# Output gates in 96 packets, constants made by GpSimd, the first weight fold in eight pieces, two PSUM accumulator tiles, and new ranks

## The chip, the cores and the metric

The kernel runs on one core of one Trainium2 chip. The metric is the device time of one execution in microseconds (us); the median of three runs is what a change is measured by. Engines are named as in the profile: PE (TensorE matmul), PEld (its weight loads), DVE (VectorE), ACT (ScalarE), POOL (GpSimd) and SP (SyncE, whose queue issues every DMA of this kernel).

## The reference, cut to what matters

```python
for t in range(S):                      # B=4, H=8, S=768, D=40
    m_new = np.maximum(f_gate[:, :, t] + m, i_gate[:, :, t])
    C = f_stab * C + i_stab * outer(vt, kt)
    n = f_stab * n + i_stab * kt
    y[:, :, t] = sigmoid(o_gate) * (C @ qt) / np.maximum(np.abs(n @ qt), 1.0)
x = y as (3072 tokens, 320)
h1 = ((x @ w1) * (x @ w2)) @ w3 @ w_out          # d_ff 1024
out = maximum(h1 @ u1, h1 @ u2, h1 @ u3) @ u_out # d_ff 768
```

The weights come as 64-bit floats; attention inputs and the output are 32-bit.

## The kernel before, in words

The recurrence is done in chunks of L = 87 steps, nine per batch (the last has 72): within a chunk, products of q, k and v are weighted with a matrix of decays. The two feed-forward layers run on blocks of 384 tokens, eight in all, behind the chunks that make their tokens. Every matrix product of the layers is made of several matmuls on a high part and a low part of each operand.

**The order of the work** is made by a planner written into the kernel (class Plan). Every step is entered with its engine, an assumed cost in ns, a function that issues its instructions, and what it reads and writes. Each step has a rank in the list PRIO, the n-th number for the n-th step entered; when an engine is free, the ready step with the lowest rank goes next. PICK holds a digit for every step that may run on either of two engines. The result is a fixed program for each engine, SP's queue of DMAs too. WARM is the planner's assumed time up to which matmuls take twice as long; it issues nothing. A DMA is held back in the plan while what it has issued is more than AHEAD (2500 ns) ahead by the plan's costs. On the chip, each engine runs its program in order and waits for what an instruction needs.

**The start**, which the change touches:

- *Gates* (L477 to L563): one DMA brings the input and forget gates as 32 rows (L477). DVE runs a chain over them: scan (L491), subtraction (L502), scan (L506), short scan (L515), maximum (L521). The result of batch 0 is written to a scratch in device memory (L529, called dna0 below) and read back in another layout (L561, called rv), which SP can issue only once dna0 has landed. ACT (L562) and DVE (L563) make the high and low part hl1 of it. Until both are there, no decay matrix can be made.
- *Constants*: the identity, a mask and selectors (cs, 128 rows of 97) come by DMA from an array made on the host (L478), and so do an identity with a triangle of -1e30 (sel, 96 rows of 216, L479), which ACT copies to the tile one (L535).
- *Output gates*: those of the first five chunks come in one DMA (L579) of 480 rows of 1280 B; ACT makes five sigmoids of them (L582). Every exponential of the decays is entered behind all five, since both need ACT's function table.
- *Weights* come in granules: 512 columns of 128 rows, 64-bit, 512 KB each (L1050). ACT makes the high word (L1055), DVE or ACT the middle (L1061, L1064), and DVE joins them to 32 bits (L1072). Granules go through staging buffers: four sx and three stg while the start lasts. A granule can only be loaded when the one before it in its buffer is converted.
- *Folds*: w3 @ w_out is computed first, in eight folds of 128 rows. wof (five granules wo0 to wo4) is needed by all; each fold takes two granules of w3, called w3(f,0) and w3(f,1). A fold is eight products of 128x128 by 128x320 (L1122), entered as two PE steps of four products, and each product has two records in the trace. ACT and DVE then take the fold to wb (L1129, L1133). Folds 0 and 1 stand ahead of the first decay matrix, and fold 2 and the later ones among the chunks.
- *Decay matrices* (L656, L657): two PSUM tiles per chunk, from hl0, hl1 and one; ACT takes the exponential (L660). Then the products of q and k (L738) and of the weighted matrix with v (L747). PSUM tiles wk are three, used in turn by folds and decay matrices in the order entered: fold 2 has to wait for the exponential of a decay matrix of chunk 0.
- *PSUM accumulators*: one tile acs of 1536 columns is used as three accumulators ac0, ac1 and ac2.

From some 30 us on PE works without a pause through chunks, folds and layers.

Of the kernel before, what the change touches and what calls it, by code (L numbers as in the profile page):

```python
# [62 lines left out]
    "10110100100101010111000001100000100101110111110011010011011011100000111101110010111101010110110010011011100100"  # L63
    "11001010111110011110111010001110001001001110111100010011101010011011010101001000010010000000101101101100100110"
    "10000010011111110010010100111100001110000101011001101011000010100000100010111000111001100111100101000100000011"
    "01011010010011011110000111101100011011110011011100010000"
)
PRIO = (
# [286 lines left out]
def mlstm_moe_kernel(  # L355
# [10 lines left out]
    wc: bass.AP,  # L366
    wcr_in: bass.AP,
    wo2: bass.AP,
    cst: bass.AP,
    sel: bass.AP,  # L370
    out: bass.AP,
):
# [76 lines left out]
    def T(*key):  # L449
        return made[key]  # L450
# [892 lines left out]
```

## Time and profile before

| | us |
|---|---|
| median of three runs | 674.73 |
| the three runs | 671.27, 674.73, 675.07 |
| the profiled execution | 675.12 |
| its span, first to last instruction | 673.4 |
| PE busy in it | 652.2 (97%) |
| DVE, ACT, POOL busy | 358.1, 297.8, 190.3 |
| DMA | 76.09 MB, mean 113 GB/s |

Busy time of PE counts a matmul at half clock as long as it takes. Idle time of an engine that isn't the bottleneck costs nothing; what is to be read is where PE isn't busy, or is slow.

### The profile page before, as it was taken

How to read it: one execution, taken by the hardware profiler on the slowest of the kernel's cores; microseconds unless marked ns; L12 is line 12 of the kernel's file. 1: busy time of each engine (PE TensorE's matmuls, PEld its weight loads, DVE VectorE, ACT ScalarE, POOL GpSimd, SP SyncE). 2: the span in 40 equal slices, each digit the busy share in tenths (PEclk: the TensorE clock that was granted, in tenths of full speed). 3: DMA queues.
4: the chain of work that ended last, by engine and by line, in shares of the span. 5: the costliest groups of instructions: out<-in, count | busy, mean ns of one | idle time of the engine just before them, and what ended most of it. 6: DMA issues, size and time to landing. Idle time of an engine off the chain costs nothing. (4 is left out here: it accounts for less than half of the span.)

```text
span 673.4 us, 14869 instructions
## 1 busy us (share of the span) xinstructions
PE 652.2 (97%) x6217; PEld 618.1 (92%) x6217; DVE 358.1 (53%) x715; ACT 297.8 (44%) x576; POOL 190.3 (28%) x193
## 2 busy tenths in 40 slices
PE   2899999999999999999999999999999999999997
PEld 1577899999999999999999999999999999999997
DVE  7578989869644563444534563455424652313231
ACT  5847977676724334342324343443334332313032
POOL 1034356234323344230312353341413220011011
PEclk9899999999999999999999999999999999999999
DMA  8989863636223352222103352221313200000001
GB/s 304 339 322 343 302 230 108 207 120 198 80 85 114 95 170 85 85 84 84 49 37 115 97 170 82 85 85 34 95 42 113 64 31 1 1 1 0 1 5 55
DMA packets 25908, 76.09 MB, mean 113 GB/s; under 512 B 3273, under 2 KB 6921, under 8 KB 25842
## 3 DMA queue, kind: packets, MB, share of 16 engines
q1 hardware_dynamic: 25842, 75.15, 33.8%
q8 instruction: 48, 0.79, 0.5%
q14 instruction: 18, 0.15, 0.1%
HBM read 71.11 MB, written 4.03 MB: 112 GB/s over the span
## 5 line engine op out<-in xcount | busy, mean ns | idle before, releaser
L888 POOL TENSOR_TENSOR pl<-misc,ph 128x384 fp32r<-128x384 f32 (+1 forms) x57 | 59.7, 1049 | 202.3 <-ACT ph L884 196.4
L884 ACT CAST ph<-misc 128x384 fp32r<-128x384 f32 (+1 forms) x114 | 57.7, 508 | 127.1 <-PE acs L986 51.6
L934 DVE TENSOR_TENSOR misc<-misc,wk 128x384 f32<-128x384 f32 (+1 forms) x98 | 53.1, 544 | 107.2 <-PE wk L862 86.1
L857 PE MATMUL wk<-xh,wch 128*128 128x384 f32 x288 | 98.3, 341 | 0.4 <-ACT misc L931 0.3
L858 PE MATMUL wk<-xh,wcl 128*128 128x384 f32 x288 | 96.9, 336 | 0.0
L859 PE MATMUL wk<-xl,wch 128*128 128x384 f32 x288 | 96.9, 336 | 0.0
L857 PE MATMUL wk<-xh,wah 128*128 128x384 f32 x256 | 87.9, 343 | 0.4 <-ACT dd L660 0.2
L859 PE MATMUL wk<-xl,wah 128*128 128x384 f32 x256 | 86.2, 337 | 0.0
L858 PE MATMUL wk<-xh,wal 128*128 128x384 f32 x256 | 86.2, 337 | 0.0
L905 DVE TENSOR_TENSOR misc<-misc,wk 128x384 f32<-128x384 f32 x64 | 35.2, 550 | 79.7 <-ACT misc L903 51.2
L903 ACT COPY misc<-wk 128x384 f32<-128x384 f32 x64 | 30.5, 478 | 70.4 <-PE wk L862 43.7
L888 DVE TENSOR_TENSOR pl<-misc,ph 128x384 fp32r<-128x384 f32 (+1 forms) x57 | 34.4, 603 | 48.7 <-ACT ph L884 48.1
L857 PEld LDWEIGHTS wk<-xh,wch 128*128 128x128 f32 x288 | 54.1, 188 | 2.6 <-ACT misc L931 0.9
L1122 PE MATMUL wk<-wof,w 128*128 128x320 f32 x128 | 41.4, 478 | 13.5 <-DVE w L1072 13.1
L858 PEld LDWEIGHTS wk<-xh,wcl 128*128 128x128 f32 x288 | 54.1, 188 | 0.0
L859 PEld LDWEIGHTS wk<-xl,wch 128*128 128x128 f32 x288 | 54.1, 188 | 0.0
L986 PE MATMUL acs<-wd,ph 128*128 128x320 f32 x288 | 51.1, 311 | 0.6 <-ACT misc L1028 0.5
L931 ACT COPY misc<-wk 128x384 f32<-128x384 f32 x48 | 23.1, 480 | 64.5 <-PE wk L862 52.4
L857 PEld LDWEIGHTS wk<-xh,wah 128*128 128x128 f32 x256 | 48.0, 188 | 2.2 <-DVE xl L839 0.7
L1122 PEld LDWEIGHTS wk<-wof,w 128*128 128x128 f32 x128 | 25.7, 208 | 25.4 <-DVE w L1072 13.9
L860 PE MATMUL wk<-xh,wcr 128*128 128x384 f32 x144 | 48.4, 336 | 0.0
L858 PEld LDWEIGHTS wk<-xh,wal 128*128 128x128 f32 x256 | 48.1, 188 | 0.0
(144 smaller groups left out, 1335.7 us busy)
## 6 DMA issues: line engine op xcount, KB each, us to landing
kv<-in_kv SPq DMA_DIRECT2D x32, 672.0 KB, 5.1
raw<-in_qk SPq DMA_DIRECT2D x36, 348.0 KB, 4.1
dd<-d_na SPq DMA_DIRECT2D x24, 348.0 KB, 3.8
stg<-in_wc SPq DMA_DIRECT2D x9, 512.0 KB, 4.6
stg<-in_w3t SPq DMA_DIRECT2D x8, 512.0 KB, 8.8
sx<-in_w3t SPq DMA_DIRECT2D x8, 512.0 KB, 8.2
out<-misc SPq DMA_DIRECT2D x24, 160.0 KB, 1.8
sx<-in_wa SPq DMA_DIRECT2D x6, 512.0 KB, 8.8
```

The source lines that it names most:

```text
L857: PE.matmul(p, lhsT=h_[:, kt], rhs=xh[:, kt], start=kt == 0, stop=False)
L858: PE.matmul(p, lhsT=l_[:, kt], rhs=xh[:, kt], start=False, stop=False)
L859: PE.matmul(p, lhsT=h_[:, kt], rhs=xl[:, kt], start=False, stop=False)
L860: PE.matmul(p, lhsT=r_, rhs=xh[:, 2], start=False, stop=False)
L884: P.op("A", act(n), lambda sl=sl: A.copy(out=T("ph", key)[:, sl], in_=T(*src)[:, sl]), r=[src + part], w=[("ph", key) + part])
L888: e.tensor_tensor(out=T("pl", key)[:, sl], in0=T(*src)[:, sl], in1=T("ph", key)[:, sl].bitcast(F32), op=ALU.subtract)
L903: P.op("A", act(TB, True), lambda: A.copy(out=T(*sa), in_=T(*ps[0])), r=[ps[0]], w=[sa])
L905: P.op("V", dve(TB), lambda: V.tensor_tensor(out=T(*sa), in0=T(*sa), in1=T(*ps[1]), op=ALU.mult), r=[ps[1]], w=[sa])
L931: P.op("A", act(TB, True), lambda: A.copy(out=T(*sc), in_=T(*ps)), r=[ps], w=[sc])
L934: P.op("V", dve(sl.stop - sl.start), lambda sl=sl: V.tensor_tensor(out=T(*sc)[:, sl], in0=T(*sc)[:, sl], in1=T(*ps)[:, sl], op=ALU.max), r ...
L986: PE.matmul(T(f"ac{m}", (k, 1)), lhsT=src[:, m * 128:m * 128 + 128], rhs=w[:, o:o + DM], start=first_, stop=last_,)
L1122: PE.matmul(T(*ps), lhsT=T(*w3)[:, i * 128:i * 128 + 128], rhs=wof[:, gt * 320:gt * 320 + 320], start=gt == 0, stop=gt == 7,)
```

## The change

- The DMAs of cst and sel, and ACT's copy to one, are gone. Two steps on POOL make cs (a memset and four affine selects) and one (a memset and two affine selects).
- The output gates of the first five chunks lie in device memory as 96 rows of 6400 B; the DMA's assumed cost is 1700 ns in place of 2500.
- The DMA of the gates has an assumed cost of 2200 ns of the queue (with its end 1300 ns sooner than that), in place of 900.
- The granule w3(0,0) is split into two halves of 256 columns, here w3a and w3b, and fold 0 is entered as eight PE steps of one product, each waiting for the granules that it reads.
- ac2 has a PSUM tile of its own; ac0 and ac1 stay in acs.
- WARM goes from 18000 to 15500; PRIO and PICK are new throughout (1963 steps before, 1972 after).

```diff
-WARM = 18000
+WARM = 15500
...
-    acs = psum.tile([128, 1536], F32, name="acs")
-    for i in range(3):
-        slots[f"ac{i}"] = [acs[:, i * 512:i * 512 + 512]]
+    acs = psum.tile([128, 1024], F32, name="acs")
+    slots.update(ac0=[acs[:, 0:512]], ac1=[acs[:, 512:1024]], ac2=[psum.tile([128, 512], F32, name="ac2")])
...
-    dma(900, lambda: SP.dma_start(out=both[:, :, 0:S], in_=gi), w=[("g", "gft"), ("g", "git", 0)])
-    dma(250, lambda: SP.dma_start(out=cs, in_=cst[:, 0:L + 1 + NCH]), w=[("cs", 0)])
-    dma(300, lambda: SP.dma_start(out=T("cr", 0), in_=sel), w=[("cr", 0)])
+    P.op("D", 2200, lambda: SP.dma_start(out=both[:, :, 0:S], in_=gi), w=[("g", "gft"), ("g", "git", 0)],
+         early={(("g", "gft"), None): 1300, (("g", "git"), 0): 1300})
+    def pick(out, in_, cm, base, pattern, op, fill):
+        G.affine_select(out=out, in_=in_, pattern=pattern, compare_op=op, fill=fill, base=base, channel_multiplier=cm)
+    def f():
+        G.memset(cs, 0.0)
+        pick(cs[:, 0:L], cs[:, 0:L], 1, 0, [[-1, L]], ALU.not_equal, 1.0)
+        pick(cs[:, L:L + 1], cs[:, L:L + 1], -1, L - 1, [[0, 1]], ALU.is_ge, 1.0)
+        e = cs[:, L + 1:L + 1 + NCH]
+        for o in (64, 96):
+            pick(e, e, 1, -o, [[-1, NCH]], ALU.not_equal, -1.0)
+    P.op("G", 1200, f, w=[("cs", 0)])
+    def f():
+        one, low = T("one", 0)[:, 0:128], T("one", 0)[:, 128:128 + LE]
+        G.memset(T("one", 0).bitcast(F32), 0.0)
+        pick(one, one.bitcast(F32), 1, 0, [[-1, 128]], ALU.not_equal, 1.0)
+        pick(low, low.bitcast(F32), -1, 0, [[1, LE]], ALU.is_ge, -1e30)
+    P.op("G", 900, f, w=[("one", 0)])
...
-    dma(2500, lambda: SP.dma_start(out=sg0[0:LP], in_=og.rearrange("c p d -> p c d")),
+    dma(1700, lambda: SP.dma_start(out=sg0[0:LP].rearrange("p c d -> p (c d)"), in_=og),
...
-            granule(w3t[ft][:, q * 512:q * 512 + 512], (w3, lambda w3=w3: T(*w3)))
...
-            P.op("P", 2150, f, cols=5120, r=[*(("wo", 0, i) for i in ((0, 1, 2), (2, 3, 4))[q]), w3], w=[ps])
+            n = 256 if (ft, q) == (0, 0) else 512
+            for o in range(0, 512, n):
+                part = (o // n,) if n < 512 else ()
+                granule(w3t[ft][:, q * 512 + o:q * 512 + o + n],
+                        (w3 + part, lambda w3=w3, o=o, n=n: T(*w3)[:, o:o + n]))
+            m = 1 if ft == 0 else 4
+            for g0 in range(q * 4, q * 4 + 4, m):
+                gts = range(g0, g0 + m)
+                wos = sorted({x // 512 for gt in gts for x in (gt * 320, gt * 320 + 319)})
+                P.op("P", 537.5 * m, lambda w3=w3, q=q, gts=gts: products(w3, q, gts), cols=1280 * m,
+                     r=[*(("wo", 0, i) for i in wos), w3 + ((g0 // 2,) if n < 512 else ())], w=[ps])
```

Ranks of the first DMAs and of the gate chain, by counting through PRIO in the order in which the steps are entered:

| step | rank before | rank after |
|---|---|---|
| gates, wo0, wo1, wo2, wo3, wo4 | 60, 81, 101, 107, 114, 118 | 75, 76, 111, 160, 161, 168 |
| w3(0,0); after: w3a, w3b | 94 | 142, 149 |
| w3(0,1), w3(1,0), w3(1,1) | 116, 104, 130 | 121, 70, 190 |
| sel, cst | 112, 122 | none |
| dna0, rv | 84, 92 | 31, 84 |
| output gates, q and k of chunk 0 | 137, 138 | 177, 180 |
| DVE: scan L491, scan L506, L515, maximum L521 | 25, 1, 5, 18 | 239, 186, 134, 81 |
| DVE, joining (L1072) wo0, wo1, wo2 | 91, 106, 358 | 68, 263, 58 |
| DVE, joining w3(0,0); after: w3a, w3b | 121 | 248, 20 |
| POOL: making cs, making one | none | 196, 27 |

## Rows read from the trace of the kernel before

**Rows 1.** The page: busy time, and the span in 40 slices.

```profile
PE 652.2 (97%) x6217; PEld 618.1 (92%) x6217; DVE 358.1 (53%) x715; ACT 297.8 (44%) x576; POOL 190.3 (28%) x193
...
PEclk9899999999999999999999999999999999999999
DMA  8989863636223352222103352221313200000001
```

**Rows 2.** Who waited for whom, PE (us in total, times, longest).

```profile
PE wk L1122 <- DVE w L1072: 13.1, 2, 12.6
PE wk L656 <- DVE hl L563: 1.7, 1, 1.7
```

**Rows 3.** Timeline of PE: start us, us, line, tiles, records, idle before and releaser.

```profile
12.57 4.63 PE L1122 MATMUL wk<-wof,w 128*128 128x320 f32 x8 [12.57 <-DVE w L1072]
17.45 4.63 PE L1122 MATMUL wk<-wof,w 128*128 128x320 f32 x16 [0.24 <-DVE wof L1072]
22.65 2.42 PE L1122 MATMUL wk<-wof,w 128*128 128x320 f32 x8 [0.56 <-DVE w L1072]
26.73 0.43 PE L656 MATMUL wk<-hl,hl 128*128 128x352 f32 x1 [1.66 <-DVE hl L563]
...
29.87 4.63 PE L1122 MATMUL wk<-wof,w 128*128 128x320 f32 x8
```

**Rows 4.** Windows: length, busy us of each engine, then PEclk, DMA share, GB/s.

```profile
0.00:12.57 12.57, 0.00 (x0) 0.00 (x0) 8.78 (x12) 6.04 (x9) 1.93 (x10) 1.00 0.82 273
12.57:26.73 14.16, 11.69 (x33) 6.81 (x33) 7.98 (x14) 12.88 (x22) 0.00 (x0) 1.00 1.04 336
...
35.00:668.40 633.40, 631.64 (x6150) 605.16 (x6148) 337.11 (x682) 272.31 (x535) 187.62 (x182) 1.00 0.31 101
668.40:673.40 5.00, 0.71 (x3) 0.44 (x3) 0.00 (x0) 1.18 (x3) 0.00 (x0) 0.95 0.28 98
```

**Rows 5.** Windows of 1 us, 27 to 35 us, the same columns.

```profile
27.00:28.00 1.00, 1.00 (x12) 0.78 (x13) 0.90 (x3) 1.00 (x3) 0.00 (x0) 0.91 1.00 409
28.00:29.00 1.00, 0.98 (x13) 0.79 (x11) 1.00 (x4) 0.98 (x2) 0.00 (x0) 0.50 1.03 411
...
33.00:34.00 1.00, 1.00 (x4) 0.61 (x3) 0.05 (x1) 0.00 (x0) 0.00 (x0) 0.50 1.01 400
34.00:35.00 1.00, 1.00 (x4) 0.79 (x4) 0.00 (x0) 0.01 (x1) 0.00 (x0) 0.67 1.04 424
```

**Rows 6.** DMA packets of two stretches: 12 to 15 us, then 17 to 21 us.

```profile
DMA packets 375, 1.22 MB, mean 406 GB/s; under 512 B 81, under 2 KB 81, under 8 KB 375
...
DMA packets 516, 0.82 MB, mean 206 GB/s; under 512 B 33, under 2 KB 398, under 8 KB 516
```

**Rows 7.** Timeline of SP's DMA issues, 10 to 18 us.

```profile
10.74 0.36 SPq L529 DMA_DIRECT2D d_na<-misc  x1
...
12.32 0.43 SPq L579 DMA_DIRECT2D sg<-in_og  x1
17.23 0.31 SPq L561 DMA_DIRECT2D misc<-d_na  x1
```

**Rows 8.** Timeline of ACT, 8 to 26 us.

```profile
8.59 0.66 ACT L1055 ACTIVATE stg<-stg 128x512 f32<-128x512 f32 x1 [1.68 <-DMA stg<-in_w3t]
...
20.65 0.67 ACT L1061 ACTIVATE sx<-sx 128x512 int32<-128x512 uint16 x1 [0.32 <-DMA sx<-in_w3t]
...
23.48 1.19 ACT L582 ACTIVATE sg<-sg 96x320 f32<-96x320 f32 x3 [0.31 <-DMA sg<-in_og]
...
25.00 0.77 ACT L562 CAST hl<-misc 9x696 fp32r<-9x696 f32 x1
```

**Rows 9.** Timeline of DVE, 7 to 27 us.

```profile
7.68 1.77 DVE L506 TENSOR_TENSOR_SCAN misc<-misc 32x783 f32<-32x783 f32 x1
...
9.75 0.96 DVE L521 TENSOR_TENSOR misc<-misc,mp 32x783 f32<-32x783 f32 x1
...
11.85 0.67 DVE L1072 SCALAR_TENSOR_TENSOR w<-stg 128x512 int32<-128x512 int32 x1
...
25.80 0.88 DVE L563 TENSOR_TENSOR hl<-misc,hl 9x696 fp32r<-9x696 f32 x1 [0.23 <-ACT hl L562]
```

**Rows 10.** Timeline of POOL, 1 to 7 us.

```profile
1.03 0.68 POOL L533 MEMSET hl<- 64x704 f32 x1
6.14 0.74 POOL L498 MEMSET misc<- 32x783 f32 x1 [4.43 <-DVE misc L491]
```

**Rows 11.** Groups of POOL by form: its affine selects before.

```profile
L679 POOL TENSOR_SCALAR_AFFINE_SELECT dd<-dd 87x696 f32<-87x696 f32 x24 | 20.7, 862 | 38.8 <-ACT dd L676 35.6 <-DMA stg<-in_wc 3.1
```

More of the change, by code (lines that the diff above doesn't have):

```diff
@@ L62 @@
 PICK = (
[L63 to L66, printed above, removed]
+    "01110000010000000000101101110001101110001110101011101011101110110111110111101101001100101110111101111010000110"
+    "01010000111010100100110001000000111101111011110000100111110111010111111010000000001100110000101111001100110010"
+    "01000111011000100011111011000001011110000001101101000001101101110001110111110000101110001111000111110001110011"
+    "001100111010101011000011110011000000111101111000011101000"
 )
 PRIO = (
[95 rows of a table removed]
[95 rows of a table added]
 )
-WARM = 18000
+WARM = 15500
 USTEPS = (0, 1, 3, 5, 9, 13, 17, 21, 25)
@@ L368, in mlstm_moe_kernel @@
     wo2: bass.AP,
-    cst: bass.AP,
-    sel: bass.AP,
     out: bass.AP,
@@ L466, in mlstm_moe_kernel @@
         o += n
-    made["rv", 0], made["cr", 0] = misc[:, 0:8 * L], misc[0:LP, o:o + 128 + LE]
+    made["rv", 0] = misc[:, 0:8 * L]
     for tag, (x, y) in where.items():
@@ L470, in mlstm_moe_kernel @@
             over[tag].append(("rv", 0))
-        if x < o + 128 + LE and o < y:
-            over[tag].append(("cr", 0))
     def c3(t):
         return t.rearrange("p (c t) -> p c t", t=L)
-    dma(900, lambda: SP.dma_start(out=both[:, :, 0:S], in_=gi), w=[("g", "gft"), ("g", "git", 0)])
-    dma(250, lambda: SP.dma_start(out=cs, in_=cst[:, 0:L + 1 + NCH]), w=[("cs", 0)])
-    dma(300, lambda: SP.dma_start(out=T("cr", 0), in_=sel), w=[("cr", 0)])
+    P.op("D", 2200, lambda: SP.dma_start(out=both[:, :, 0:S], in_=gi), w=[("g", "gft"), ("g", "git", 0)],
[16 more added lines that the diff above has]
+    P.op("G", 900, f, w=[("one", 0)])
     def f():
@@ L533, in mlstm_moe_kernel @@
     P.op("G", 400, lambda: G.memset(T("hl", 1)[64:128].bitcast(F32), 0.0), w=[("hl", 1, 2), ("hl", 1, 3)])
-    P.op("A", act(128 + LE), lambda: A.copy(out=T("one", 0), in_=T("cr", 0)[0:L]), r=[("cr", 0)], w=[("one", 0)])
     P.op("A", act(NCH * 128), lambda: A.copy(
@@ L1114, in fold, with products @@
         ps = new(("wk", ("fold", ft)), [128, 320], F32, "wk")
+        def products(w3, q, gts):
+            for gt in gts:
+                i = gt - q * 4
+                PE.matmul(
+                    T(*ps), lhsT=T(*w3)[:, i * 128:i * 128 + 128], rhs=wof[:, gt * 320:gt * 320 + 320],
+                    start=gt == 0, stop=gt == 7,
+                )
         for q in range(2):
             w3 = new(("w3", (ft, q)), [128, 512], F32, "w3")
-            granule(w3t[ft][:, q * 512:q * 512 + 512], (w3, lambda w3=w3: T(*w3)))
-            def f(q=q, w3=w3):
-                for i in range(4):
-                    gt = q * 4 + i
-                    PE.matmul(
-                        T(*ps), lhsT=T(*w3)[:, i * 128:i * 128 + 128], rhs=wof[:, gt * 320:gt * 320 + 320],
-                        start=gt == 0, stop=gt == 7,
-                    )
-            P.op("P", 2150, f, cols=5120, r=[*(("wo", 0, i) for i in ((0, 1, 2), (2, 3, 4))[q]), w3], w=[ps])
+            n = 256 if (ft, q) == (0, 0) else 512
[9 more added lines that the diff above has]
+                     r=[*(("wo", 0, i) for i in wos), w3 + ((g0 // 2,) if n < 512 else ())], w=[ps])
         w = wb[:, ft]
@@ L1303, in _lay @@
     w3 = i["moe_w3"].reshape(8, 128, 8, 128).transpose(0, 3, 2, 1).reshape(8, 128, 1024)
-    cst = np.zeros((128, 128), f)
-    cst[:, 0:L] = np.eye(128, L)
-    cst[L:R, L] = 1.0
-    cst[64:64 + NCH, L + 1:L + 1 + NCH] = cst[96:96 + NCH, L + 1:L + 1 + NCH] = -np.eye(NCH)
-    sel = np.eye(LP, 128 + LE, dtype=f)
-    sel[:, 128:] = np.where(np.arange(LP)[:, None] > np.arange(LE), f(-1e30), f(0))
     return {
@@ L1313, in _lay @@
         "kv": kvw,
-        "og": og[0, 0:SIGN],
+        "og": og[0, 0:SIGN].transpose(1, 0, 2).reshape(LP, SIGN * DM),
         "w3t": w3,
@@ L1321, in _lay @@
         "wo2": i["moe2_w_out"].reshape(6, 128, 320),
-        "cst": cst,
-        "sel": sel,
     }
```

190 rows, old and new, of the table PRIO are left out of this document.

## The prediction, made before the result was known

> **What bounds the kernel now.** I read the page first: PE is busy 97% of the span, the next engine 53% [rows 1]. Then the windows, cut at the places where PE's timeline changes. From 35 us to the last matmuls PE is busy 631.64 us of 633.40, so 1.8 us of idle time is all that a better order could win there; the last 5 us are the output leaving [rows 4]. What can be won lies in the first 35 us. The list of waits says what ends PE's idle time there: joined weights for 13.1 us and hl1 for 1.7 us [rows 2]. The timeline shows it in order: first matmul at 12.57, folds 0 and 1 to 25.07 with gaps of 0.24 and 0.56, a gap of 1.66 for hl1, the first decay matrix at 26.73 [rows 3].
>
> Two stretches of PE are slow besides. Eight records of a fold take 4.63 us at 12.57 and again at 29.87, where sixteen take 4.63 us at 17.45: half rate [rows 3]. The first slow stretch is how PE starts after its long idle time (the clock column reads 1.00 there, so I go by the records); it costs 4.63 / 2 = 2.3 us. The second is a fall of the granted clock: 0.91 in the window from 27 us, 0.50 in the six from 28 to 34, 0.67 in the next [rows 5]. Its loss is 0.09 + 6 x 0.50 + 0.33 = 3.4 us. Before it PE had idled 0.56 and 1.66 us within five microseconds [rows 3].
>
> So the end is: the time from which PE is fed without a gap, plus the work left, plus the half-clock losses. I call the first of these the feed point; before, it is 26.73. It needs two things: fold 1 finished (its last granule w3(1,1)), and hl1 (gates, dna0, rv). PE starting sooner is worth nothing alone: folds 0 and 1 then only wait in the middle. Both chains run through the DMA queue, which is full from 12.57 to 26.73 (share 1.04) [rows 4].
>
> **Output gates.** Between 17 and 21 us the engines are as busy as before but move 206 GB/s in place of 406 [rows 6]. In those 4 us 16 engines have 64 us. The 118 packets of 2 KB or more are rows of weights or of q and k; at 406 / 16 = 25.4 GB/s one of 4096 B takes 161 ns, so they take at most 19 us. The 398 smaller ones, nearly all output gates of 1280 B, share the other 45 us: 113 ns each, against 50 ns by their bytes. All 480 take 480 x 113 / 16 = 3.4 us. As 96 packets of 6400 B at 25.4 GB/s, 252 ns each, they take 1.5 us. The gain is 1.9 at most, and 0 if the slow stretch has another cause than packet length (480 x 50 / 16 is 1.5 us too). I take 1.7, since the slow stretch is where these packets are.
>
> The Trainium skill ("DMA: Bandwidth & Descriptors", section "Why small descriptors are slow (HBM only)") speaks against this: a packet carries a fixed overhead of about 3 cycles beside one for every 32 B. By that, 1280 B cost 43 cycles in place of 40 and 6400 B cost 203 in place of 200, so the gain is an estimated 0.1 us. The rows (113 ns against 50) don't agree.
>
> **Constants.** The DMAs of sel and cst go: 129.5 KB and 224 packets. By bytes at 406 GB/s that is 0.3 us of the queue, by 113 ns a packet 1.6. Between 12 and 15 us 81 packets under 512 B passed while the rate stayed at 406 [rows 6], so I take 0.7, nearer the low end. POOL makes them in its idle time: it has nothing from 1.71 to 6.14 [rows 10]. An affine select of 696 columns takes 862 ns [rows 11]; the six have 322 columns together, so 0.4 us if columns set the time, and 5.2 us if each costs as much as the long one. The memsets of 97 and 216 columns are under the 0.68 us that 704 columns took [rows 10]. At worst 6.6 us: POOL's memset for the second scan, at 6.14, would come near 8.3 and that scan (at 7.68 [rows 9]) 1.4 us later. I take 0 on the path, bounds 0 and 1.4 on the gate chain. The copy on ACT that goes is off the path too.
>
> **The gates' DMA at 2200 ns.** It moves the same bytes. In the plan it holds the granules behind it back by 1.3 us, about one granule, so less stands in the queue when dna0 is issued. Before, dna0 was issued at 10.74 and rv, which waits for its landing, at 17.23 [rows 7]: 6.5 us, mostly queue. Bounds for dna0: 0 (if the plan's hold isn't what limits SP) and 1.3 sooner. I take 1.3, since the queue is full throughout.
>
> **The fold in pieces.** The arithmetic is the same, 64 products. Before, ACT had w3(0,0) from 8.59 on [rows 8], DVE joined it only at 11.85, behind the gate chain [rows 9]. After, the first product needs wo0 and half a granule. I put its start at 10.8, between 9.8 (ACT begins the half at 8.6, then 1.2 us of halved steps) and 12.6 (as before). Half a granule more means one more set of instructions: two on ACT and one or two on DVE, 0 to 2 us of these engines, beside DMA time; I take 0. From 10.8, four products at half rate (4.63) and twelve at full rate (12 x 0.58 = 6.9) end at 22.4, so PE itself no longer sets the end of fold 1.
>
> **The feed point.** Fold 1's end: ACT took w3(1,1) on its landing, 20.65 [rows 8], and PE ended 4.4 later, 25.07. Ahead of it go 1.7 (gates) and 0.7 (constants), but its rank is now 190, behind 177 (output gates) and 180 (q and k of chunk 0): 348 KB at 406 GB/s come in front, +0.9. So 25.07 - 1.7 - 0.7 + 0.9 = 23.6. hl1: ready at 25.80 + 0.88 = 26.68 [rows 9]. ACT had stood before it at the sigmoids, which waited for the output gates' DMA until 23.48 [rows 8]. dna0 lands 1.3 + 0.7 sooner, and rv and the output gates behind it 1.7 more: 26.68 - 3.7 = 23.0. The later of the two is 23.6, rounded to 23.5: the feed point moves by -3.2. If the bounds of the parts are all at their poor end (gates 0, constants 0.3, hold 0), fold 1 ends at 25.7 and hl1 comes near 26.4: -0.3. If they are at the good end, and w3(1,1) isn't held back, PE's own 22.4 sets it: -4.3.
>
> **The clock.** With fold 1 ending at 23.6 and hl1 there at 23.0, the gap of 1.66 is gone, and I take the fall at 27.9 as gone with it: -3.4, bounds 0 and -3.4. One of the three runs before is 3.5 us under the median, about this price; it may be a run without the fall, which no row shows.
>
> **The rest.** PSUM in two tiles and WARM issue nothing: 0. New ranks change every engine's order; against the 1.8 us idle after 35 us [rows 4] they can win at most that, and lose as much again where one buffer turns late. I take 0, bounds -1.5 and +2.
>
> Sum: 675.12 - 3.2 - 3.4 = **668.5 us**, from the profiled execution, which lies 0.4 over the median of 674.73. It is 0.9% under that median. A measurement of this kernel can tell about 1% from no change: 668.0 and 681.5 are the bounds.
>
> **Rivals.**
> - *The clock falls all the same* (25%). For it: PE still starts late, and short decay matrices still follow fold 1. Against it: less idle time just before. 675.12 - 3.2 = 671.9.
> - *The slow stretch isn't the packets* (12%), as by the rule above. Then fold 1 ends at 25.07 - 0.7 + 0.9 = 25.3, and the feed point moves by -1.4; with the fall of the clock still there, 673.7. Against it is the rate, which halves just where these packets are.
> - *The gate chain is pushed back* (8%), the slower side. Its scans now rank 239 and 186 and its maximum 81, behind the joins of w3b (20), wo2 (58) and wo0 (68). Four joins at 0.67 us [rows 9] put dna0 2.7 us later, and every 1.3 us lets another granule into the queue ahead of it, so rv 5.3 later. Less the 3.7 won, hl1 is ready at 28.3; PE idles longer after fold 1 and the clock falls: 675.12 + 1.6 = 676.7. It decides from dna0 issued about 1.9 us later than before, at 12.6. Against it: DVE is free when the gates land, and a scan, once started, runs.
> - *Better than forecast* (10%): w3(1,1) isn't held back and the feed point is PE's own 22.4: 675.12 - 4.3 - 3.4 = 667.4.
>
> **Numbers.** The forecast holds 45%. Its own spread of 1.5 us puts a third of it below 668.0; with most of the better rival that makes 27% faster. Slower than 681.5 needs the pushed chain and worse ranks: 3%. The rest, 70%, is within 1%. The range reaches from the forecast less 3 (the better rival and ranks that win 1.5 more) over the clock and packet rivals to 675.0; outside it lie most of the slower rival and the tails.
>
> **What would show it.** First matmul near 10.8; the output gates' stretch at 350 GB/s or more; rv issued near 15; the first decay matrix near 23.5 with less than 0.5 us idle before it; PEclk at 1.0 from 25 to 35 us; PE's idle time after 35 us still below 3 us. The forecast is wrong if the clock column shows 0.50 after the folds, if dna0 is issued after 12.6, or if PE waits anew after 35 us.

## The result, and the profile after

| | before | after |
|---|---|---|
| median, us (runs of one comparison) | 674.62 (6) | 669.03 (6) |
| lowest and highest | 671.27, 676.19 | 667.69, 669.27 |
| the profiled execution | 675.12 | 669.1 |
| its span | 673.4 | 667.4 |

The ratio is 0.9919, with a 95% interval of 0.9895 to 0.9943: the change wins 5.6 us, where 6.2 were forecast. In two later comparisons the same kernel gave 0.9881 (0.9856 to 0.9906) and 0.9937 (0.9915 to 0.9960).

The page of the kernel after, beside [rows 1]: busy time, and the clock column of the 40 slices.

```profile
PE 647.3 (97%) x6217; PEld 617.8 (93%) x6217; DVE 364.9 (55%) x730; ACT 293.8 (44%) x568; POOL 186.9 (28%) x196
...
PEclk9999999999999999999999999999999999999999
```

PE does the same 6217 matmuls in 4.9 us less, and the dip in the clock's second slice is gone. PE's timeline of the kernel after, to be laid beside [rows 3]:

```profile
12.39 2.10 PE L584 MATMUL ac<-cs,misc 32*127 32x32 f32 x9 [12.39 <-DVE misc L540]
14.42 4.64 PE L1132 MATMUL wk<-wof,w 128*128 128x320 f32 x8
19.21 5.21 PE L1132 MATMUL wk<-wof,w 128*128 128x320 f32 x16 [0.16 <-DVE w L1086]
24.01 0.56 PE L670 MATMUL wk<-hl,hl 128*128 128x352 f32 x1
...
25.78 2.42 PE L1132 MATMUL wk<-wof,w 128*128 128x320 f32 x8
```

From 12.39 us on PE hardly pauses. Nine small products of the gate chain now stand first on PE; the folds follow, with one gap of 0.16. The first decay matrix starts at 24.01, 2.7 sooner than before, with no idle time noted ahead of it, where 1.66 was. Fold 1 no longer ends ahead of it: its second half comes behind, at 25.78. The clock stays whole where [rows 5] had 0.50:

```profile
28.00:29.00 1.00, 1.00 (x6) 0.80 (x5) 1.00 (x3) 0.76 (x3) 0.57 (x1) 1.00 1.11 377
...
33.00:34.00 1.00, 1.00 (x17) 0.77 (x18) 0.56 (x2) 1.00 (x3) 0.00 (x0) 1.00 1.02 422
```

SP's issues, beside [rows 7], and below them two rows of ACT's timeline, beside [rows 8]:

```profile
10.67 0.34 SPq L544 DMA_DIRECT2D d_na<-misc  x1
11.06 0.34 SPq L593 DMA_DIRECT2D sg<-in_og  x1
...
14.90 0.30 SPq L575 DMA_DIRECT2D misc<-d_na  x1
...
18.14 0.47 ACT L596 ACTIVATE sg<-sg 96x320 f32<-96x320 f32 x1 [1.02 <-DMA sg<-in_og]
...
21.10 0.77 ACT L576 CAST hl<-misc 9x696 fp32r<-9x696 f32 x1
```

dna0 is issued as early as before (10.67 against 10.74), but rv 4.2 us behind it in place of 6.5, and ACT's part of hl1 comes at 21.10 in place of 25.00. POOL makes the constants from 0.81 to 2.67 us:

```profile
0.81 0.27 POOL L490 MEMSET one<- 87x216 f32 x1 [0.29 <-POOLq L1346]
1.16 0.51 POOL L476 TENSOR_SCALAR_AFFINE_SELECT one<-one 87x128 fp32r<-87x128 f32 x2
1.62 0.18 POOL L479 MEMSET cs<- 128x97 f32 x1
1.86 0.81 POOL L476 TENSOR_SCALAR_AFFINE_SELECT cs<-cs 128x87 f32<-128x87 f32 x4
```

Last, PE's waits after the first matmul. One of 1.5 us is new, at 134 us:

```profile
PE wk L871 <- ACT misc L917: 1.5, 1, 1.5
PE wk L670 <- ACT dd L674: 0.6, 1, 0.6
PE acs L985 <- POOL pl L902: 0.6, 1, 0.6
```

To see where the 6.0 us between the two profiled executions lie I took, for each of PE's records, the time to the start of the next, less the median of that time for the same two kinds of matmul. The excess in the first 50 us falls from 10.1 to 4.7 us; behind 50 us it goes from 25.7 to 25.0. So the gain is made at the start, as forecast, and the long rest looks untouched. That second reading did not survive the experiments. Even in this trace the rest is two changes that nearly cancel: split once more at 140 us, the excess rises by some 3 us between 50 and 140 and falls by some 4 behind. And by the windows PE's idle time from 35 to 662 us is 3.6 us, where it was 1.7.

### The profile page after: what moved, and what is told of

Its sections match the earlier page's. It is cut to its first block, busy times and chain, and to the rows that moved or that the text cites. A ratio compares the mean times of both kernels' runs of the same rounds, so it can differ in the third digit from the quotient of the medians.

```text
span 667.4 us, 14865 instructions
## 1 busy us (share of the span) xinstructions
PE 647.3 (97%) x6217; PEld 617.8 (93%) x6217; DVE 364.9 (55%) x730; ACT 293.8 (44%) x568; POOL 186.9 (28%) x196
## 4 chain that ended last, share of the span: by engine, by line
PE 89%; DVE 4%; ACT 3%; DMA 2%; issue 1%; SPq 0%; POOL 0%; ACTq 0%; DVEq 0%; POOLq 0%
PE wk L871 14%; PE wk L872 13%; PE wk L873 13%; PE wk L874 7%; PE acs L1000 6%; PE wk L876 5%; PE aq L761 3%; PE wk L1132 3%; PE ac L1000 3%; PE acs L985 3%; PE acs L981 3%; PE acs L983 3%; PE aq L752 3%; PE wk L832 2%; PE ac L985 2%; PE wk L886 2%
## 5 line engine op out<-in xcount | busy, mean ns | idle before, releaser
L902 POOL TENSOR_TENSOR pl<-misc,ph 128x384 fp32r<-128x384 f32 (+1 forms) x55 | 57.9, 1053 | 219.2 <-ACT ph L898 218.5
L872 PE MATMUL wk<-xh,wcl 128*128 128x384 f32 x288 | 97.1, 337 | 0.0
L872 PE MATMUL wk<-xh,wal 128*128 128x384 f32 x256 | 86.3, 337 | 0.0
L902 DVE TENSOR_TENSOR pl<-misc,ph 128x384 fp32r<-128x384 f32 (+1 forms) x59 | 35.8, 608 | 38.9 <-ACT ph L898 38.5
L872 PEld LDWEIGHTS wk<-xh,wcl 128*128 128x128 f32 x288 | 54.2, 188 | 0.0
L872 PEld LDWEIGHTS wk<-xh,wal 128*128 128x128 f32 x256 | 48.1, 188 | 0.0
L873 PEld LDWEIGHTS wk<-xl,wah 128*128 128x128 f32 x256 | 48.1, 188 | 0.0
L985 PE MATMUL acs<-pl,wb 128*128 128x384 f32 x128 | 43.2, 338 | 0.6 <-POOL pl L902 0.6
L1000 PE MATMUL acs<-wd,ph 128*128 128x320 f32 x192 | 43.2, 310 | 0.0
```

Source lines behind the costliest of these rows:

```text
L872: PE.matmul(p, lhsT=l_[:, kt], rhs=xh[:, kt], start=False, stop=False)
L873: PE.matmul(p, lhsT=h_[:, kt], rhs=xl[:, kt], start=False, stop=False)
L902: e.tensor_tensor(out=T("pl", key)[:, sl], in0=T(*src)[:, sl], in1=T("ph", key)[:, sl].bitcast(F32), op=ALU.subtract)
L985: PE.matmul(a, lhsT=w[:, o:o + 128], rhs=l_, start=False, stop=sp)
L1000: PE.matmul(T(f"ac{m}", (k, 1)), lhsT=src[:, m * 128:m * 128 + 128], rhs=w[:, o:o + DM], start=first_, stop=last_,)
```

## The experiments

Nine edited kernels, one of them twice, and the kernel after as a control, twice, ran in three sets, each set on one chip with its own runs of the kernel before. Ratios are to those. Line numbers shift by a few between kernels. I count a run as having the fall of the clock when its mean granted clock is below 0.9975: the two profiled executions with the fall have 0.995 and 0.997, all those without it 0.998 or more.

**Is it the gap that lets the clock fall?** In the kernel before, three products that nobody reads fill PE's wait for hl1.

```diff
+                if (ft, q) == (1, 1):
+                    for x in range(3):
+                        PE.matmul(
+                            acs[:, 1024:1344], lhsT=T(*w3)[:, 0:128], rhs=wof[:, 0:320], start=True, stop=True,
+                        )
```

> The kernel before, with three more fold products (six records, 1.7 us at full rate) put on PE behind fold 1, into an accumulator that nothing reads; they fill the idle 1.66 us before the first decay matrix. Theory (the fall of the clock at 27.9 us follows from PE's idle time before it): no window at 0.50 after 27 us, 3.4 us less than the kernel before, near 671.2. Rival (the fall comes from the short decay and attention matmuls behind the gap, or from something outside the kernel): the fall stays, the time stays within 0.5 us of 674.6.

673.35 us, ratio 0.9997 (0.9978 to 1.0015). The first decay matrix now follows without a wait, and shorter waits come behind it:

```profile
24.23 1.78 PE L1128 MATMUL acs<-wof,w 128*128 128x320 f32 x6
25.70 0.48 PE L656 MATMUL wk<-hl,hl 128*128 128x352 f32 x1
...
27.85 0.40 PE L656 MATMUL wk<-hl,hl 128*128 128x352 f32 x1 [0.40 <-DVE wb L1138]
...
28.86 2.42 PE L1122 MATMUL wk<-wof,w 128*128 128x320 f32 x8 [0.45 <-ACT dd L660]
```

The fall is gone: in each of the 10 runs the mean granted clock is above 0.9975. Of the 29 runs of the kernel before beside them 14 are below that; their median is 674.6, and 672.6 that of the other 15. So the gap is what lets the clock fall, but in half of the runs only, and a run with the fall costs 2 us more than one without. Filling the gap gave no time, against the 3.4 us expected: the runs lie 0.7 above those of before without the fall. Why they aren't faster stays open, since the first decay matrix comes 1.0 sooner.

**Does a late hl1 bring the gap back?** In the kernel after, DVE makes the low part of hl1 five times over.

```diff
-    P.op("V", dve(8 * L), lambda: V.tensor_tensor(
-        out=T("hl", 1)[96:96 + NCH, :, 0:L], in0=raw_v, in1=hi.bitcast(F32), op=ALU.subtract
-    ), r=[("rv", 0), ("hl", 1, 2)], w=[("hl", 1, 3)])
+    def f():
+        for _ in range(5):
+            V.tensor_tensor(
+                out=T("hl", 1)[96:96 + NCH, :, 0:L], in0=raw_v, in1=hi.bitcast(F32), op=ALU.subtract
+            )
+    P.op("V", dve(8 * L), f, r=[("rv", 0), ("hl", 1, 2)], w=[("hl", 1, 3)])
```

> The changed kernel, with DVE's last step of hl1 done five times over instead of once (the same values), so that hl1 comes 3.5 us later, at about 26.3, and PE idles some 2.2 us before the first decay matrix at 24.0. Theory (idle time there makes the clock fall): +2.2 for the gap and +3.4 for a fall, near 674.5, with six to seven windows at 0.50. Rival (the fall isn't made by the gap): +2.2 alone, near 671.2, clock 1.0 throughout. If DVE's delay is hidden by fold 1's last products: +0.

674.39 us, ratio 1.0018 (0.9995 to 1.0041): all of the gain is lost. PE's timeline:

```profile
26.75 0.40 PE L674 MATMUL wk<-hl,hl 128*128 128x352 f32 x1 [2.84 <-DVE hl L579]
```

A gap of 2.84 us, and the first decay matrix where it was before the change. Here 7 of 10 runs have the fall, with a median of 675.32; the other three, of which the profiled one is one, lie at 671.13 to 672.25. The gap alone costs some 3 us (671.24 against the 668.33 of the next kernel, on the same chip), and the fall 4 on top.

**What are the 96 packets worth?** The kernel after with the output gates as 480 packets again.

```diff
-    dma(1700, lambda: SP.dma_start(out=sg0[0:LP].rearrange("p c d -> p (c d)"), in_=og),
+    dma(1700, lambda: SP.dma_start(out=sg0[0:LP], in_=og.rearrange("c p d -> p c d")),
```

> The changed kernel, with the output gates of the first five chunks as 480 rows of 1280 B again; order, ranks and everything else as changed. The prediction's term (packet length makes the slow stretch, 1.7 us of the queue): the output gates land 1.7 us later and the feed point moves by at least 1 us, so 670 or more. Theory after reading the trace after (96 packets of 402 ns against 480 of 96 ns, 2.4 us against 2.9): the queue gains 0.5 us only, and PE waits for neither: within 0.3 us of 669.0.

668.33 us, ratio 0.9925 (0.9903 to 0.9947), beside the change's 0.9919: worth nothing. The DMA's packets from 13 to 17 us, first of the kernel after, then of this one:

```profile
DMA packets 266, 1.01 MB, mean 254 GB/s; under 512 B 75, under 2 KB 75, under 8 KB 266
```

```profile
DMA packets 636, 1.00 MB, mean 251 GB/s; under 512 B 72, under 2 KB 542, under 8 KB 636
```

With 370 packets more the same bytes pass at the same rate. In the trace a packet of 1280 B takes 75 ns here and one of 6400 B takes 402 ns in the kernel after: 480 x 75 / 16 = 2.3 us of the queue against 96 x 402 / 16 = 2.4. These times differ between traces: reckoned the same way, 480 short packets take 2.3 to 2.9 us in four kernels and 96 long ones 2.0 to 2.5 in four others, so at most a few tenths are in it.

**What is it worth that POOL makes the constants?** The kernel after with cs and sel by DMA, and ACT's copy to one, in place of POOL's steps.

```diff
+    cr = big.tile([LP, 128 + LE], F32, name="cr")
...
+        SP.dma_start(out=both[:, :, 0:S], in_=gi)
+        SP.dma_start(out=cs, in_=cst[:, 0:L + 1 + NCH])
+        SP.dma_start(out=cr, in_=sel)
...
+        A.copy(out=T("one", 0), in_=cr[0:L])
```

> The changed kernel, with cs and the identity with its triangle brought by DMA again, issued right behind the gates' DMA, and copied by ACT before its hl0 step; order and ranks as changed. Theory (the constants' DMAs are 0.5 us of the queue, and PE is held from 12 to 19 us by joins on DVE): within 0.5 us of 669.0. Rival (making them early on POOL is what lets ACT do its 2.7 us of hl0 and hl1 copies before the first weights land): ACT waits for the landing, converts wo0 some 1.5 us later, and the time rises by 1 to 2 us, to 670 to 671.

671.02 us, ratio 0.9960 (0.9944 to 0.9976): 2.7 us over the run with 480 packets, on the same chip. The same kernel was run again in the third set, beside a control:

> The changed kernel with its constants loaded by two DMAs again, beside a control. My theory: the copies of ScalarE that turn cs into the first gate operands and wo0 come 1.5 us later, everything behind them too, so the first decay matrix stands near 24.2 us or later and the time is 2.0 to 2.7 us above the control. Rival: the 2.7 us measured before against the run with the output gates in 480 packets were partly that run's, and against the control it is under 1 us.

671.38 us, ratio 0.9968 (0.9953 to 0.9982), against 668.66 for the control: 2.7 again. But the mechanism that I had put down is only half there. ACT's timeline of the control, then of this kernel:

```profile
2.70 1.15 ACT L550 CAST hl<-cs 64x1152 fp32r<-64x1152 f32 x1 [0.61 <-POOL cs L476]
```

```profile
4.38 1.15 ACT L539 CAST hl<-cs 64x1152 fp32r<-64x1152 f32 x1 [2.29 <-DMA cs<-in_cst]
```

ACT does start 1.7 us later. Yet the first decay matrix came at 23.89, not later than the control's 24.61, and what PE lost it lost at 50 us, behind a granule that landed late (ACT's row first):

```profile
47.13 0.67 ACT L1059 ACTIVATE sx<-sx 128x512 f32<-128x512 f32 x1 [1.71 <-DMA sx<-in_w3t]
...
50.00 1.31 PE L1122 MATMUL wk<-wof,w 128*128 128x320 f32 x4 [1.08 <-DVE wb L1145]
```

The other run of this edit has no such wait: there the first decay matrix comes at 24.22, against 23.77 in the kernel with 480 packets. So how the late start of ACT becomes time is not shown, only that both runs lose 2.7 us.

A further 1.4 us (1.7 in the first run of the pair) is lost behind 140 us without any wait: there the mean time from one matmul on xh and wc to the next is 175.7 ns, against 174.1 in the kernel after and 174.4 in the one before, which also loaded its constants. Both runs of this edit show it, the controls don't. The edit needs a place in SBUF for sel, which it takes as a tile of its own; before, sel lay in a buffer that was used again. Whether that placing slows the matmuls was not tried. So the constants made on POOL are worth between 1.0 and 2.7 us, the lower number if the slower matmuls belong to the experiment.

**The control of the second set**, the kernel after unedited:

> The changed kernel as it is, as a control beside the next three on the same chip: 669.0, within 0.5, and the clock at 0.998 or more in every run.

666.99 us, ratio 0.9881 (0.9856 to 0.9906); no run has the fall, where 10 of the 15 of before beside it have (674.94 against 673.12).

**What do the parts win without the new ranks?** The kernel before, with its ranks, its assumed costs and its undivided fold, but with the output gates in 96 packets, the constants from POOL and the two PSUM tiles. The plan keeps the steps that are gone, with nothing to issue.

```diff
+    acs = psum.tile([128, 1024], F32, name="acs")
+    slots.update(ac0=[acs[:, 0:512]], ac1=[acs[:, 512:1024]], ac2=[psum.tile([128, 512], F32, name="ac2")])
...
+    dma(250, lambda: None, w=[("cs", 0)])
+    dma(300, lambda: None, w=[("cr", 0)])
...
+        G.memset(T("hl", 1)[64:128].bitcast(F32), 0.0)
+        make_one()
+        make_cs()
...
+    dma(2500, lambda: SP.dma_start(out=sg0[0:LP].rearrange("p c d -> p (c d)"), in_=og),
```

> The kernel before with its old order and ranks, but with the output gates in 96 packets, the constants made by POOL behind its first memsets (and the two DMAs and ACT's copy gone), and ac2 in a PSUM tile of its own: the parts without the new order and without the split fold. Theory (the order makes the gain: hl1 comes earlier because less is queued ahead of dna0 and the output gates): old order, so the gap before the first decay matrix shrinks by 1 us at most; within 1.5 us of the kernel before, 672 to 674, and some runs still with a fall of the clock. Rival (the parts themselves make it): 670 or less, no falls.

671.61 us, ratio 0.9942 (0.9923 to 0.9962): 3.2 of the 7.8 us that the control of this set wins. PE's timeline:

```profile
12.60 10.89 PE L1143 MATMUL wk<-wof,w 128*128 128x320 f32 x32 [12.60 <-DVE w L1093]
24.66 0.40 PE L677 MATMUL wk<-hl,hl 128*128 128x352 f32 x1 [1.16 <-DVE hl L584]
...
27.73 3.44 PE L1143 MATMUL wk<-wof,w 128*128 128x320 f32 x7 [0.28 <-ACT dd L681]
```

The folds run without a gap, 24.66 is 2.1 sooner than before, but hl1 is still waited for, and the clock still falls: seven records of a fold take 3.44 us where the kernel after has seven in 2.05 at 28.36. Nine of the ten runs have the fall. That the gap goes is the work of the new order. The two waits for accumulators that PE has in the kernel before (0.5 us each) are not in this trace; what the two tiles alone are worth in the old order was not tried.

**Would PE gain from a whole run of folds?** In the kernel after, DVE makes the low part of hl0 (L571, 1.35 us) behind the joining of w3(0,1), which PE waits for within fold 0.

```diff
+    kept = []
...
-        t, h = aug()
-        V.tensor_tensor(out=h[32:64], in0=t, in1=h[0:32].bitcast(F32), op=ALU.subtract)
+        def g():
+            t, h = aug()
+            V.tensor_tensor(out=h[32:64], in0=t, in1=h[0:32].bitcast(F32), op=ALU.subtract)
+        kept.append(g)
...
+            if i == 7:
+                kept.pop()()
```

> The changed kernel, with DVE's step hl0 lo (1.35 us, needed at 24 us) moved behind the joining of w3(0,1), which PE waits for at 19.2. Theory (from 14 to 19 us PE is held by DVE's joins): w3(0,1) is joined some 1.3 us sooner, PE's second half of fold 0 starts near 18.0, and the end comes 0.5 to 1.2 us sooner, 667.8 to 668.5. Rival (the next granule, w3(1,0), or the slow clock takes its place): within 0.3 us of the changed kernel.

667.15 us, ratio 0.9886 (0.9858 to 0.9914): the control's time. The folds close up, and nothing comes of it:

```profile
14.56 9.51 PE L1139 MATMUL wk<-wof,w 128*128 128x320 f32 x24
23.67 0.56 PE L675 MATMUL wk<-hl,hl 128*128 128x352 f32 x1
```

The first decay matrix stands at 23.67, as in the control (23.62). hl1 isn't what it waits for, which is complete at 22.96; PE comes from the folds. The control's folds, and below them those of this kernel from a window that starts at 20.4 us:

```profile
14.65 4.64 PE L1132 MATMUL wk<-wof,w 128*128 128x320 f32 x8
19.45 4.57 PE L1132 MATMUL wk<-wof,w 128*128 128x320 f32 x16 [0.16 <-DVE w L1086]
```

```profile
20.06 4.01 PE L1139 MATMUL wk<-wof,w 128*128 128x320 f32 x14
```

In the control eight records run at half rate and sixteen at full rate. Here ten do the first 5.50 us, from 14.56 to 20.06, and fourteen the rest: what the closed gap gives, two more slow records take. That is the slow clock of the rival.

**Can the new wait at 134 us go?** In the kernel after, the exponential that ACT issues there moves behind the copy that PE waits for.

```diff
+        js = [j for t, j, fn in order]
+        late = order.pop(js.index(506))
+        js = [j for t, j, fn in order]
+        order.insert(js.index(493) + 1, late)
```

> The changed kernel, with one exponential of a decay matrix (chunk 12) moved on ACT behind the high-word copy of x and the copy of a product that PE waits for at 134 us (1.55 us idle). Theory (the wait is ACT's order behind a late subtraction on DVE): the wait goes down to 0.3 to 0.5 us and the end comes 1.0 us sooner, near 668.0. Rival (what PE gains it loses at the next buffer): within 0.3 us of the changed kernel.

665.77 us, ratio 0.9863 (0.9835 to 0.9891): 1.2 us under the control, as expected, and the fastest of all the kernels here. ACT and PE of the kernel after:

```profile
132.41 0.78 ACT L690 ACTIVATE dd<-dd 127x696 f32<-127x696 f32 x1 [1.88 <-DVE dd L684]
...
133.50 0.47 ACT L917 COPY misc<-wk 128x384 f32<-128x384 f32 x1
...
134.02 0.45 PE L871 MATMUL wk<-xh,wah 128*128 128x384 f32 x1 [1.55 <-ACT misc L917]
```

ACT stands for 1.88 us at an exponential whose input is late, with the copy that PE needs behind it. With the two exchanged the copy runs at once, and the exponential, off the path, still comes sooner than before. PE's wait is gone:

```profile
129.88 0.47 ACT L921 COPY misc<-wk 128x384 f32<-128x384 f32 x1
130.37 1.28 ACT L694 ACT_TABLE_LOAD   x1
131.66 0.79 ACT L694 ACTIVATE dd<-dd 127x696 f32<-127x696 f32 x1
...
132.21 0.34 PE L875 MATMUL wk<-xh,wah 128*128 128x384 f32 x1
```

**The control of the third set:**

> The changed kernel, nothing edited, as the control of the three others on the same chip. By every theory 666.5 to 669.3 us, which is what it took so far, with no fall of the granted clock between 25 and 35 us and the first decay matrix at 23.5 to 24.2 us.

668.66 us, ratio 0.9937 (0.9915 to 0.9960). Of the 29 runs of before beside it 13 have the fall (674.45), the others 672.68.

**Do the two PSUM tiles do anything?** The kernel after with the three accumulators in one tile.

```diff
-    acs = psum.tile([128, 1024], F32, name="acs")
-    slots.update(ac0=[acs[:, 0:512]], ac1=[acs[:, 512:1024]], ac2=[psum.tile([128, 512], F32, name="ac2")])
+    acs = psum.tile([128, 1536], F32, name="acs")
+    for i in range(3):
+        slots[f"ac{i}"] = [acs[:, i * 512:i * 512 + 512]]
```

> The changed kernel with the three accumulators of PSUM in one tile of 1536 columns, as before. My theory, as in the prediction: the two tiles issue nothing and spare no wait, so the time is the control's within 0.5 us. Rival: a tile of its own for the third accumulator spares a wait on the bank's other users, and one tile costs 1 us or more, seen as more idle time of TensorE.

673.44 us, ratio 1.0000 (0.9981 to 1.0020). My theory falls: this one edit is worth 4.8 us, nearly the whole gain. Not one instruction differs between the two kernels, and the start is as good (first decay matrix at 23.79). One of its 12 runs has a mean clock of 0.995, which no trace explains. What differs is who waits for whom. The groups, by form, of the instructions that read the accumulators, in the control (count, busy us, mean ns, idle before and its releaser):

```profile
L1026 DVE TENSOR_TENSOR xl<-acs,xh 128x384 fp32r<-128x384 f32 x16 | 8.5, 551 | 10.1 <-ACT xh L1022 10.0
...
L1018 ACT COPY misc<-ac 64x384 f32<-64x384 f32 x8 | 3.8, 477 | 0.3
```

and in this kernel:

```profile
L1027 DVE TENSOR_TENSOR xl<-acs,xh 128x384 fp32r<-128x384 f32 x16 | 8.9, 554 | 16.1 <-ACT xh L1023 8.7 <-ACT misc L1020 7.5
...
L1019 ACT COPY misc<-acs 64x384 f32<-64x384 f32 x8 | 3.8, 476 | 3.5 <-DVE xl L1027 3.2 <-PE acs L986 0.2
```

L1027 reads ac0 or ac1, L1019 and L1020 read ac2. In one tile DVE waits 7.5 us for ACT's copies of another accumulator, and ACT's copies 3.2 us for DVE. In two tiles neither wait is there. One case, in the control, where ACT's second copy of ac2 runs from 126.11 to 126.58 and DVE reads beside it (DVE's rows first, then ACT's):

```profile
126.16 0.55 DVE L1026 TENSOR_TENSOR xl<-acs,xh 128x384 fp32r<-128x384 f32 x1
...
126.11 0.47 ACT L1019 COPY misc<-ac 64x384 f32<-64x384 f32 x1
```

and with one tile, where DVE and ACT take turns and PE waits for the last reader of all three before it starts the next ac0:

```profile
126.26 0.56 DVE L1027 TENSOR_TENSOR xl<-acs,xh 128x384 fp32r<-128x384 f32 x1 [0.56 <-ACT misc L1020]
...
125.27 0.48 ACT L1019 COPY misc<-acs 64x384 f32<-64x384 f32 x1 [0.72 <-DVE xl L1027]
...
127.42 0.76 PE L982 MATMUL acs<-ph,wb 128*128 128x384 f32 x3 [0.42 <-DVE misc L1035]
```

Followed record by record, the one-tile kernel falls behind the control in eight steps of 0.3 to 1.0 us between 127 and 663 us: four at a first product into an accumulator (L982, L1001), the others where the copy of a finished product comes late (L872).

**What do the new ranks win alone?** The kernel after with constants by DMA, 480 packets and one PSUM tile, so the three edits above together.

> The changed kernel with the constants by DMA, the output gates in 480 packets and one PSUM tile, so that the new ranks and the fold in pieces alone are left. My theory: of the three parts undone only the constants count, so the time is that of the run with the constants by DMA within 0.7 us, 2.0 to 2.7 above the control, and the ranks carry what is left against the kernel before, 3 to 5 us. Rival: the parts add up to the 3.2 us that they were worth in the old order, or more, and the time is 3.2 us or more above the control.

675.00 us, ratio 1.0029 (1.0014 to 1.0045): no run has the fall, the first decay matrix is at 24.39, and still it is no faster than before. The rival holds: this is 6.3 us over the control, less than the two parts that count took one by one (2.7 + 4.8), but more than the 3.2 that all three won in the old order. It has the slower matmuls behind 140 us as well (175.6 ns). PE's waits:

```profile
PE wk L862 <- ACT misc L908: 1.4, 1, 1.4
PE acs L972 <- DVE misc L1025: 0.9, 1, 0.9
```

So the new ranks without the parts win 2.3 us at the start and the clock, and lose that and 1.4 us more later on.

## Why the prediction was right in its sum, and where its terms were not

- **What bounds the kernel.** Right as to the start: PE's first 35 us held what the order could win, and the page, the waits and the windows led there. PE's idle time before the first decay matrix (1.66) went, and so did the fall. But the bound of 1.8 us on what lies behind 35 us was read from the old order alone: with one tile the new order loses 4.8 us there, and one exchange at 134 us wins 1.2.
- **The feed point, -3.2.** Measured 26.73 to 24.01 in the profile, -2.7; 23.6 to 24.6 in other runs of the kernel. Right within 0.5, though not by its steps. Fold 1's end doesn't set it any more, since the new order puts fold 1's second half behind the decay matrices. hl1 comes when reckoned (its last part ends at 22.8, forecast 23.0), but isn't waited for in this profile: PE itself is at the folds until 24.0. In the control of the third set hl1 comes at 24.47 and is what sets 24.61.
- **The clock, -3.4.** The mechanism is shown from both sides: filling the gap before took the fall away (0 of 10 runs against 14 of 29), and a late hl1 after brought it back (7 of 10). The size was taken from one profiled execution that had the fall. Between runs of the kernel before with and without it the difference is 2 us, and only half of the runs have it. So the median wins about 1 us by this, not 3.4. The remark that the quickest of the three runs may be one without the fall fits these runs.
- **The gates' DMA, -1.3 for dna0.** Wrong: 0.1. dna0 was issued at 10.67 in place of 10.74, so the plan's hold isn't what limits SP there. hl1 came 3.9 sooner all the same, 2.3 of it because dna0 landed sooner and rv could go at 14.90; the kernel with the parts in the old order has 1.8 of these 2.3 (rv at 15.42). That hl1 agrees with the forecast, whose terms were 1.3, 0.7 and 1.7, is luck.
- **Output gates, -1.7 of queue.** Wrong: 0. The step that failed divided the slow stretch's time by its small packets, and so took a slow stretch where the packets are for one because of them. With 96 long packets that stretch is as slow as with 480 short ones (254 GB/s, 251). The 113 ns a packet, reckoned as a remainder, was high besides: the trace of before has 96. The estimate of 0.1 us that the prediction worked out from the Trainium skill ("DMA: Bandwidth & Descriptors", section "Why small descriptors are slow (HBM only)") was nearer, and the traces agree that length matters little: 2.3 us of the queue with short packets, 2.4 with long ones. What slows the stretch stays open. Its packets fill 96 rows of SBUF and the weights' 128; that was not tried.
- **Constants, -0.7 by the queue, POOL at 0.** POOL's side is right: its six selects take 1.3 us, between the bounds of 0.4 and 5.2, and nobody waits. The gain is larger than the term, 1.0 to 2.7 us, and comes by another way: ACT's first operands are ready 1.7 us sooner. How that reaches the end is not shown; the two runs without it lose at different places.
- **First product at 10.8.** It came at 14.42. Half a granule was joined at 11.37, but the new order puts nine products of the gate chain first, whose input is ready at 12.24. Fold 0's second half can't start before w3(0,1) is joined at 19.16, so an earlier start would in the main move the wait into the middle, as argued. It isn't shown to be free: the sixteen records behind that wait take 5.21 us where sixteen at full rate take 4.57, so PE's slow start reaches into them.
- **PSUM and WARM, 0; ranks, 0.** The sum of the two was near, each alone far off. "PSUM in two tiles issues nothing: 0" is the step that failed: it asked what the edit issues, not what waits on the tile. With the new order the two tiles are worth 4.8 us. And the new order alone isn't 0 either: without the parts, the excess of PE behind 50 us that I reckoned above is 29.3 us, against 25.7 in the order of before. The trace of the kernel before could have raised the question. In its list of PE's waits, under [rows 2], stand

```profile
PE acs L967 <- DVE misc L1020: 0.5, 2, 0.3
PE acs L986 <- ACT misc L1028: 0.5, 1, 0.5
```

waits for accumulators by first products into them. I passed them over as small.
- **The rivals.** The clock fell in no run of the kernel after. The gate chain was not pushed back: dna0 went at 10.67, and its point of decision was 12.6. That the slow stretch isn't the packets came true, but at no cost, since fold 1's end no longer sets the feed point. PE's own work sets it, as in the better rival, but at 24.0 and not at 22.4, since the folds start at 14.42 and run slow for longer. And one of the prediction's own signs of being wrong came: PE waits anew after 35 us (1.55 at 134 us), and its idle time there is 3.6, above the 3 that it allowed.

The rule for it is in the Trainium skill ("PSUM — Partial Sum Buffer", section "PSUM bank collisions raise a hardware error"): two engines must be kept apart only where they touch the same bank and the same 32 partitions. Each accumulator here is 512 columns of 4 B, one bank of 2 KiB by that page. The traces agree: in two tiles ACT and DVE read ac2 and an accumulator of acs at the same time (126.16 us). So the waits of 7.5 and 3.2 us are those of the tile as the unit that the program orders by.

Taken together, forecast against median: feed point -2.7, clock about -1 (an estimate: 2 us in half of the runs), and a remainder of -5.6 + 3.7, some -2. No trace shows the whole remainder; in the profiled pair PE's excess behind 50 us falls by 0.7. The forecast of -6.2 was near because the clock's term was 2.4 too large and the remainder, put at 0, some 2 too small. The mechanism of the start was right; that the sum agrees is luck.

## What to carry to other kernels

An edit that issues nothing can still be worth microseconds: ask of every tile who may hold it at the same time, and give what different engines read at once tiles of their own. New ranks are worth what the buffers allow, so an order and a buffer layout are to be tried together: alone, neither the parts (3.2 of 7.8 us) nor the ranks (1.4 us slower than before) made this change. And a stretch of slow DMA is not explained by the packets in it until other packets have been sent through it.

## What the runs showed of the hardware that was not expected

- Whether the granted clock falls after PE's gap differs from run to run of one kernel. Named by the waits before or soon after the first decay matrix in its profiled execution: with 1.66 us and shorter ones, 14 of 29, 10 of 15 and 13 of 29 runs; with 2.84, 7 of 10; with 1.16 and two short ones behind it, 9 of 10; with 0.40 and 0.45 only, 0 of 10. The kernel after, with 0.16 in one profile and 0.93 and 0.55 between the folds in another, has it in 0 of 18 runs. But the one-tile kernel, with 0.16, has one low clock in 12.
- The same matmuls on the same operands take 175.6 to 175.7 ns from start to start in the three runs that hold sel in a tile of its own, and 173.8 to 174.6 in all others. Over the late stage that is 1.4 us with no wait in the trace. Its cause is open.
- The affine selects on POOL took from 0.18 us with 1 column to 0.29 with 128, where one of 696 columns takes 0.86 [rows 11]: part of the cost is fixed.
